# Linear attention and two mixture layers on one core: attention loads as four tiles four groups ahead, banks apart, weight splits in pieces

## Chip, cores and metric

One core of one Trainium2 chip. The metric is device microseconds of one execution. Five engines work from queues of their own: TensorE (PE; its weight loads are PEld), VectorE (DVE), ScalarE (ACT), GpSimd (POOL) and SyncE (SP), which here only issues transfers.

## The reference, cut to what matters

```python
for t in range(S):                                   # B, H, S, D = 4, 8, 768, 48
    cur = einsum('bhd,bhe->bhde', u * k[t], v[t])
    y[t] = einsum('bhd,bhde->bhe', r[t], state + cur)
    state = w[:, :, None] * state + einsum('bhd,bhe->bhde', k[t], v[t])
x = y.transpose(0, 2, 1, 3).reshape(3072, 384)
idx = argmax(normed(x) @ normed(expert_emb).T / tau)  # top-1 of 8 experts
out[idx == e] = gate * (relu(x[idx == e] @ w1[e]) @ w2[e])   # 384 -> 1024 -> 384
h = out @ w_in                                        # 384 -> 2048
y = (h * clip(h + 3, 0, 6) / 6) @ w_out               # 2048 -> 384
```

## The kernel before, in words

The sequence is cut into 6 chunks of 128 tokens (NCH), the 8 heads into 4 pairs (HP). A *group* is one pair of heads of one chunk for all 4 batches; there are 24, in the order of the loop at L709. Behind them come the experts, one after the other (`expert`, L473), and the last layer (L1091 on). The experts' weights are float32 and are split into a high and a low part (`prep_w`, L179: a CAST on ScalarE at L187, a subtraction at L190), so that each product is three matmuls (`mm3`, L388).

What one group i does, by helper:

- `load` (L519): two transfers by SyncE. `dt_t` (112 x 1536 floats: r, k and v with the head's dimension on the partitions) and `tk` (128 x 832: k and v with the token on the partitions). Both have three buffers.
- `scaled` (L609): `k_s` and `r_s` on VectorE, `rk_p` on GpSimd, `kk` on VectorE (not in the last chunk).
- `scores` (L622): 8 matmuls into two banks `a_ps`, copies by ScalarE (L632), a causal mask by GpSimd (L633) into `a_m`.
- `current` (L638): the matmul `m_ps` (L641), and `mv = m_ps * v` on VectorE (L643), which is the last reader of `dt_t`.
- `outputs` (L646): `y_ps` from the state (L652, not in the first chunk) and from `a_m` (L656), `u_ps` (L663), then `y_sb` (L665) and the new state (L670) on VectorE.
- `by_token` (L673): four transposes of `y_sb` into `x_ps` (L677), copied by ScalarE (L678).

In iteration i the loop issues the loads of group i+2, the scores and `m_ps` of i+1, the transposes of i-1, `scaled` of i+2 and the outputs of i. TensorE's instructions keep the order in which the program writes them (`pin`), and the others are placed by a scheduler when the program is built. Each engine works strictly in its order.

Every fourth group the routing of the chunk before is taken one step further (`route`, L203): `lt_ps` (L211), `l_ps` (L220) and a chain of small operations on VectorE that ends in `ohot` and `aft`, then ranks `r_ps` (L243 to L247) and counts `c_ps` (L251), and four scatters of rows by GpSimd (L266). At group 15 the biggest expert so far is chosen (`leader`, L317); SyncE reads its number (`lead_i`, L134) before it can ask for its weights (L173).

PSUM has 8 banks. During the attention `psM` has two, in turn for `m_ps`, `lt_ps`, `l_ps`, `r_ps`, `c_ps` and the transposes of `x_cols`; `a_ps` has two, `y_ps` two, `u_ps` and `x_ps` one each. The weights' transfers go through a staging pool of two buffers (`wst`); the first three are split at group 20 (L738).

Of the kernel before, what the change touches and what calls it, by code (L numbers as in the profile page):

```python
# [44 lines left out]
def rwkv_moe_kernel(ctx, tc, dT, tokA, wuT, uw, emb, tau, w1, w2, win, wout, out):  # L45
# [133 lines left out]
    def prep_w(j, lo_eng, after=None, st=None):  # L179
        if st is None:  # L180
            st = load_w(j)
        wp = wpools[(j // 4) % 2]
        hi = wp.tile([128, WCH], F32R, name="whi", tag="whi")
        lo = wp.tile([128, WCH], F32R, name="wlo", tag="wlo")
        for c0 in range(0, WCH, WCH // 3):
            sl = slice(c0, c0 + WCH // 3)
            cp = nc.scalar.copy(out=hi[:, sl], in_=st[:, sl])  # L187
            if after:
                behind(cp, after)
            sub = lo_eng.tensor_tensor(out=lo[:, sl], in0=st[:, sl], in1=hi[:, sl].bitcast(F32), op=ALU.subtract)  # L190
# [12 lines left out]
    def route(c, x_t, sm, xT, st_p, group="rows", pin=lambda i: i):  # L203
# [38 lines left out]
        r_ps = psM.tile([128, B, E], F32, name="r_ps", tag="m")  # L242
# [5 lines left out]
        c_ps = psM.tile([128, 2, E], F32, name="c_ps", tag="m")  # L248
# [257 lines left out]
    with actx:  # L506
        ld = actx.enter_context(tc.tile_pool(name="ld", bufs=3))
# [4 lines left out]
        yp = actx.enter_context(tc.tile_pool(name="yp", bufs=HP + 2))  # L512
# [6 lines left out]
        def load(c, hp):  # L519
            dt_t = ld.tile([112, 3, B, C], F32, name="dt_t", tag="dt")  # L520
            loads[c * HP + hp] = nc.sync.dma_start(out=dt_t, in_=dT[c, hp].rearrange("p (x b t) -> p x b t", x=3, b=B)).ins
            tk = ld.tile([128, B * 96 + B * 112], F32, name="tk", tag="tk", bufs=3)
            nc.sync.dma_start(out=tk, in_=tokA[c, hp][:, 2 * B * 96:])
            return dt_t, (tk[:, 0:B * 96].rearrange("p (b d) -> p b d", b=B), tk[:, B * 96:].rearrange("p (b d) -> p b d", b=B))
# [10 lines left out]
        for i in range(1, 2):  # L535
            data[i] = load(*groups[i])
# [72 lines left out]
        def scaled(c, hp, dt_t, tk):  # L609
            r_s = rk.tile([112, B, C], F32, name="r_s", tag="r", bufs=3)  # L610
            k_s = rk.tile([112, B, C], F32, name="k_s", tag="k")
            loads["k_s"] = nc.vector.tensor_tensor(out=k_s, in0=dt_t[:, 1], in1=itab[:, hp:hp + 1, :].to_broadcast([112, B, C]), op=ALU.mult).ins
            nc.vector.tensor_tensor(out=r_s, in0=dt_t[:, 0], in1=ptab[:, hp:hp + 1, 0:C].to_broadcast([112, B, C]), op=ALU.mult)
            rk_p = rk.tile([112, B, C], F32, name="rk_p", tag="ku")
            nc.gpsimd.tensor_tensor(out=rk_p, in0=dt_t[:, 0], in1=dt_t[:, 1], op=ALU.mult)
            kk = None
            if c < NCH - 1:
                kk = rk.tile([128, B, 96], F32, name="kk", tag="kk", bufs=3)
                nc.vector.tensor_tensor(out=kk, in0=tk[0], in1=ktab[:, hp:hp + 1, :].to_broadcast([128, B, 96]), op=ALU.mult)
            return r_s, k_s, rk_p, kk  # L620
# [17 lines left out]
        def current(c, hp, dt_t, rk_p):  # L638
# [7 lines left out]
        def outputs(c, hp, tk, r_s, a_sb, kk, mv):  # L646
            s_n, s_o = (state[hp][(c - i) % 2] for i in range(2))
            y_ps = psY.tile([112, B, C], F32, name="y_ps", tag="y")
            if c > 0:
                for b in range(B):  # L650
                    for p0, n in halves:
                        pin(nc.tensor.matmul(y_ps[p0:p0 + n, b, :], lhsT=s_o[p0:p0 + 48, b, 0:n], rhs=r_s[p0:p0 + 48, b, :],  # L652
                                             start=(b == 0), stop=False, skip_group_check=True))
            for b in range(B):
                for h2, (p0, n) in enumerate(halves):
                    pin(nc.tensor.matmul(y_ps[p0:p0 + n, b, :], lhsT=tk[1][:, b, p0:p0 + n], rhs=a_sb[h2][:, b, :],  # L656
                                         start=(c == 0), stop=True, skip_group_check=True))
# [24 lines left out]
        AHEAD = 2
# [26 lines left out]
        for i, (c, hp) in enumerate(groups):  # L709
# [12 lines left out]
            ys[i] = outputs(c, hp, data[i][1], r_s, a_sbs.pop(i), kk, mvs.pop(i))  # L722
# [6 lines left out]
            if c == KC and hp == 3:  # L729
# [468 lines left out]
```

## Time and profile before

| | |
|---|---|
| median of 3 runs | 863.66 us (862.76 to 864.56) |
| the profiled execution | 861.97 us, span 860.3 us |
| mean granted clock of TensorE | 0.962 |
| busy share of the span | PE 92%, PEld 82%, DVE 58%, ACT 39%, POOL 26% |
| first matmul of the first expert (L390) | 201.78 us |

The span begins with the first instruction. A busy share is a mean over stages with different limits, so each stage is read by itself: up to 201.78 us is the attention, behind it the experts. The clock is a share of TensorE's full speed.

### The profile page before, as it was taken

Reading aid. Unit: us, or ns where it says so; the run is one execution under the profiler, and the core shown is the slowest. Engines: PE = TensorE matmul, PEld = TensorE weight load, DVE = VectorE, ACT = ScalarE, POOL = GpSimd, SP = SyncE. Lnnn points to the kernel's source line nnn. Section 1 sums busy time; section 2 is a strip of 40 time slices with the busy share of each in tenths; the row PEclk is TensorE's granted clock in tenths of the full one; section 3 lists DMA queues with packets and bytes.
Section 4 is the critical chain, followed back from the end, with each engine's and each line's share of the span. In section 5 each row is a group of like instructions: output and inputs, shape, how many; then the busy total and the mean of one; then the engine's idle time right before and its main releaser. Section 6 shows DMA issues by size and latency. Waiting matters only on the chain. (4 is left out here: it accounts for less than half of the span.)

```text
span 860.3 us, 13475 instructions
## 1 busy us (share of the span) xinstructions
PE 792.6 (92%) x5178; PEld 703.9 (82%) x5179; DVE 495.9 (58%) x1014; ACT 331.9 (39%) x644; POOL 225.3 (26%) x239
## 2 busy tenths in 40 slices
PE   7678678598999999999999999999999999999994
PEld 4456556477899999999888998798998999998994
DVE  7764556766376778785948878744334334333331
ACT  3333132443355545564444433443333334333331
POOL 6645535564333224322110111121002002001001
PEclk8979798799999999999999999999999999999998
DMA  7556557842466465745322221111000001000000
GB/s 199 149 154 171 165 156 220 224 131 90 146 195 201 160 202 187 224 151 175 109 80 75 70 60 55 38 38 37 1 1 37 1 1 37 1 1 37 1 1 37
DMA packets 24024, 86.42 MB, mean 100 GB/s; under 512 B 3852, under 2 KB 5953, under 8 KB 23952
## 3 DMA queue, kind: packets, MB, share of 16 engines
q1 hardware_dynamic: 18784, 70.81, 27.4%
q0 software_dynamic: 5168, 14.68, 4.8%
q8 instruction: 42, 0.69, 0.3%
q14 instruction: 30, 0.25, 0.1%
HBM read 72.84 MB, written 12.63 MB: 99 GB/s over the span
## 5 line engine op out<-in xcount | busy, mean ns | idle before, releaser
L391 PE MATMUL l<-xl,whi 128*128 128x512 f32 (+8 forms) x504 | 186.8, 371 | 0.0
L390 PE MATMUL l<-xh,whi 128*128 128x512 f32 (+8 forms) x504 | 184.5, 371 | 2.0 <-DVEq L1057 1.7
L392 PE MATMUL l<-xh,wlo 128*128 128x512 f32 (+8 forms) x504 | 186.0, 370 | 0.0
L426 DVE SCALAR_TENSOR_TENSOR rg<-rg,l 128x512 f32<-128x512 f32 x96 | 65.8, 687 | 132.1 <-ACT rg L425 131.9
L425 ACT ACTIVATE rg<-l,nums 128x512 f32<-128x512 f32 x96 | 65.7, 688 | 170.8 <-PE l L392 160.2
L441 PE MATMUL o<-wlo,hh 128*128 128x384 f32 x384 | 128.7, 335 | 0.4 <-POOL wlo L1085 0.4
L440 PE MATMUL o<-whi,hh 128*128 128x384 f32 x384 | 128.1, 336 | 0.5 <-ACT hh L427 0.5
L442 PE MATMUL o<-whi,hl 128*128 128x384 f32 x384 | 123.9, 335 | 0.0
L390 PEld LDWEIGHTS l<-xh,whi 128*128 128x128 f32 x504 | 95.0, 190 | 13.4 <-issue 2.9
L392 PEld LDWEIGHTS l<-xh,wlo 128*128 128x128 f32 x504 | 95.4, 189 | 12.9
L391 PEld LDWEIGHTS l<-xl,whi 128*128 128x128 f32 x504 | 95.3, 189 | 10.1
L428 DVE TENSOR_TENSOR hl<-rg,hh 128x512 fp32r<-128x512 f32 x96 | 66.7, 696 | 43.7 <-ACT hh L427 43.1
L1115 POOL DMA_INDIRECT out_dram<-o_t,ctok x20 | 20.6, 1032 | 254.4 <-ACT o_t L1113 250.8
L427 ACT CAST hh<-rg 128x512 fp32r<-128x512 f32 x96 | 59.4, 621 | 67.4 <-DVE rg L426 52.5
L440 PEld LDWEIGHTS o<-whi,hh 128*128 128x128 f32 x384 | 72.0, 188 | 5.2 <-ACT hh L427 0.8
L441 PEld LDWEIGHTS o<-wlo,hh 128*128 128x128 f32 x384 | 72.1, 188 | 4.1 <-POOL wlo L1085 0.7
L391 PE MATMUL acc<-hl,whi 128*128 128x256 f32 (+7 forms) x216 | 71.8, 334 | 0.2 <-DVE hl L487 0.2
L392 PE MATMUL acc<-hh,wlo 128*128 128x256 f32 (+7 forms) x216 | 72.0, 335 | 0.0
L442 PEld LDWEIGHTS o<-whi,hl 128*128 128x128 f32 x384 | 71.7, 188 | 0.3
L487 DVE SCALAR_TENSOR_TENSOR hl<-l,hh 128x256 fp32r<-128x256 f32 (+7 forms) x72 | 38.1, 542 | 54.5 <-ACT hh L486 54.4
L486 ACT ACTIVATE hh<-l 128x256 fp32r<-128x256 f32 (+7 forms) x72 | 33.5, 480 | 92.5 <-PE l L392 89.7
L390 PE MATMUL acc<-hh,whi 128*128 128x256 f32 (+7 forms) x216 | 65.2, 335 | 0.7 <-DVE x L903 0.7
(215 smaller groups left out, 1191.5 us busy)
## 6 DMA issues: line engine op xcount, KB each, us to landing
wst<-in_w_dram SPq DMA_DIRECT2D x32, 768.0 KB, 4.3
dt_t<-in_dT_dram SPq DMA_DIRECT2D x24, 672.0 KB, 5.2
tk<-in_tok_dram SPq DMA_DIRECT2D x24, 416.0 KB, 5.5
q<-in_win_dram SPq DMA_DIRECT2D x16, 384.0 KB, 3.4
q<-in_wout_dram SPq DMA_DIRECT2D x16, 384.0 KB, 3.2
wf_d<-t SPq DMA_DIRECT2D x16, 192.0 KB, 4.1
wst<-wf_d SPq DMA_DIRECT2D x4, 768.0 KB, 4.6
rows<-xs_d,prod POOLq DMA_INDIRECT x27, 4.7
```

The source lines that it names most:

```text
L390: pin(nc.tensor.matmul(ps, lhsT=w[0], rhs=x[0], start=first, stop=False))
L391: pin(nc.tensor.matmul(ps, lhsT=w[0], rhs=x[1], start=False, stop=False))
L392: pin(nc.tensor.matmul(ps, lhsT=w[1], rhs=x[0], start=False, stop=last))
L425: nc.scalar.activation(out=r6, in_=ps, func=AF.Relu, bias=three)
L426: nc.vector.scalar_tensor_tensor(out=gf, in0=r6, scalar=6.0, in1=ps, op0=ALU.min, op1=ALU.mult)
L427: nc.scalar.copy(out=gh, in_=gf)
L428: nc.vector.tensor_tensor(out=gl, in0=gf, in1=gh.bitcast(F32), op=ALU.subtract)
L440: pin(nc.tensor.matmul(acc[t], lhsT=gh[:, sl], rhs=wh[:, f % 4, :], start=(f == span[0]), stop=False))
L441: pin(nc.tensor.matmul(acc[t], lhsT=gh[:, sl], rhs=wl[:, f % 4, :], start=False, stop=False))
L442: pin(nc.tensor.matmul(acc[t], lhsT=gl[:, sl], rhs=wh[:, f % 4, :], start=False, stop=(f == span[1] - 1)))
L486: last["a"] = nc.scalar.activation(out=hh[:, 0:n], in_=ps[:, 0:n], func=AF.Relu).ins
L487: last["v"] = nc.vector.scalar_tensor_tensor(out=hl[:, 0:n], in0=ps[:, 0:n], scalar=0.0, in1=hh[:, 0:n].bitcast(F32), op0=ALU.max, op1=ALU ...
```

## The change

- `load` issues four transfers a group in place of two: `rk_t` (r and k, 3 buffers), `tk` (k by token, 3), `vd` (v by dimension, 5) and `vt` (v by token, 5), with the same bytes in all. They are requested four groups ahead in place of two, the first four groups before the loop.
- `m_ps` gets a pool `psW` of one bank; `y_ps` has one bank in place of two.
- `c_ps` becomes a part of the bank of `r_ps`.
- The first four weight transfers stand behind the loads of groups 20 to 23 (before: 12 to 15). The splits of the first three chunks are nine pieces, two each at groups 18, 19, 20 and 22 and one at 23, ordered behind `x_t` on ScalarE and behind `y_sb` on VectorE.
- `yp` has one buffer fewer.

```diff
-        behind(dma, 12 + j if j < 4 else HP * NCH - 1)
+        behind(dma, (20, 21, 22, 23)[j] if j < 4 else HP * NCH - 1)
...
-        for c0 in range(0, WCH, WCH // 3):
+
+        def piece(c0):
             sl = slice(c0, c0 + WCH // 3)
             cp = nc.scalar.copy(out=hi[:, sl], in_=st[:, sl])
             if after:
...
+            if after == "x_t":
+                behind(sub, "y_s")
+        for c0 in range(0, WCH, WCH // 3):
+            if later is None:
+                piece(c0)
+            else:
+                later.append(lambda c0=c0: piece(c0))
...
-        r_ps = psM.tile([128, B, E], F32, name="r_ps", tag="m")
+        rc_ps = psM.tile([128, B + 2, E], F32, name="r_ps", tag="m")
+        r_ps, c_ps = rc_ps[:, 0:B], rc_ps[:, B:]
...
-        c_ps = psM.tile([128, 2, E], F32, name="c_ps", tag="m")
...
-        psY = pa.enter_context(tc.tile_pool(name="psY", bufs=2, space=PSUM))
+        psY = pa.enter_context(tc.tile_pool(name="psY", bufs=1, space=PSUM))
+        psW = pa.enter_context(tc.tile_pool(name="psW", bufs=1, space=PSUM))
...
-            dt_t = ld.tile([112, 3, B, C], F32, name="dt_t", tag="dt")
-            loads[c * HP + hp] = nc.sync.dma_start(out=dt_t, in_=dT[c, hp].rearrange("p (x b t) -> p x b t", x=3, b=B)).ins
-            tk = ld.tile([128, B * 96 + B * 112], F32, name="tk", tag="tk", bufs=3)
-            nc.sync.dma_start(out=tk, in_=tokA[c, hp][:, 2 * B * 96:])
...
+            rk_t = ld.tile([112, 2, B, C], F32, name="rk_t", tag="rk", bufs=3)
+            loads[c * HP + hp] = nc.sync.dma_start(out=rk_t, in_=dT[c, hp][:, 0:2 * B * C].rearrange("p (x b t) -> p x b t", x=2, b=B)).ins
+            tk = ld.tile([128, B, 96], F32, name="tk", tag="tk", bufs=3)
+            nc.sync.dma_start(out=tk, in_=tokA[c, hp][:, 2 * B * 96:3 * B * 96].rearrange("p (b d) -> p b d", b=B))
+            vd = ld.tile([112, B, C], F32, name="vd", tag="vd", bufs=5)
+            nc.sync.dma_start(out=vd, in_=dT[c, hp][:, 2 * B * C:].rearrange("p (b t) -> p b t", b=B))
+            vt = ld.tile([128, B, 112], F32, name="vt", tag="vt", bufs=5)
+            nc.sync.dma_start(out=vt, in_=tokA[c, hp][:, 3 * B * 96:].rearrange("p (b d) -> p b d", b=B))
...
-        for i in range(1, 2):
+        for i in range(1, 4):
             data[i] = load(*groups[i])
...
-            m_ps = psM.tile([112, B, C], F32, name="m_ps", tag="m")
+            m_ps = psW.tile([112, B, C], F32, name="m_ps", tag="w")
...
-            nc.vector.tensor_tensor(out=mv, in0=m_ps, in1=dt_t[:, 2], op=ALU.mult)
+            nc.vector.tensor_tensor(out=mv, in0=m_ps, in1=vd, op=ALU.mult)
...
-        AHEAD = 2
+        AHEAD = 4
...
+            if i in (16, 17, 20):
+                j = (16, 17, 20).index(i)
+                chunks[j] = prep_w(j, nc.vector, "x_t", load_w(j), pieces)
+            for _ in range((0, 0, 2, 2, 2, 0, 2, 1)[i - 16] if i >= 16 else 0):
+                pieces.pop(0)()
             if i == 20:
                 x0 = x_cols(rows0, NE, e0p, NE)
-                for j in range(3):
-                    chunks[j] = prep_w(j, nc.vector)
+            if i == 21:
                 st3 = load_w(3)
```

In the built programs the instructions move as follows (the changed kernel's line numbers are 8 to 13 higher for the same operation).

SyncE's queue, requests for loads in the middle of the attention; the number behind a tile's name tells its buffers apart. Before:

```order
L521 DMA dt_t_1176<-in_dT_dram 112x1536
L523 DMA tk_1076<-in_tok_dram 128x832
L521 DMA dt_t_1249<-in_dT_dram 112x1536
L523 DMA tk_1178<-in_tok_dram 128x832
L521 DMA dt_t_1333<-in_dT_dram 112x1536
```

With the change, at the place where the leader's number is read (`vd`, `rk_t`, `vt`, `tk` are the four parts of a group's load; `vt` is of the group before the others):

```order
L534 DMA vd_1718<-in_dT_dram 112x512
L530 DMA rk_t_1714<-in_dT_dram 112x1024
L536 DMA vt_1615<-in_tok_dram 128x448
L532 DMA tk_1716<-in_tok_dram 128x384
L134 TENSOR_LOAD lead_i_136
L134 ISA x2
L173 ISA
L173 DMA wst_1802<-in_w1_dram 128x1536
L534 DMA vd_1820<-in_dT_dram 112x512
L532 DMA tk_1818<-in_tok_dram 128x384
L530 DMA rk_t_1816<-in_dT_dram 112x1024
```

Four requests stand where two stood, the weights' first request has moved behind the loads of more groups, and the read of `lead_i` stands ahead of the parts of group 20.

VectorE, one group without routing, before:

```order
L612 TENSOR_TENSOR k_s<-dt_t,itab 112x512
L619 TENSOR_TENSOR kk<-tk,ktab 128x384
L643 TENSOR_TENSOR mv<-m_ps,dt_t 112x512
L613 TENSOR_TENSOR r_s<-dt_t,ptab 112x512
L665 TENSOR_TENSOR y_sb<-y_ps,mv 112x512
L670 SCALAR_TENSOR_TENSOR state_1_232<-state_0_231,ptab,u_ps 112x4x48
```

With the change:

```order
L632 TENSOR_TENSOR kk<-tk,ktab 128x384
L625 TENSOR_TENSOR k_s<-rk_t,itab 112x512
L656 TENSOR_TENSOR mv<-m_ps,vd 112x512
L626 TENSOR_TENSOR r_s<-rk_t,ptab 112x512
L678 TENSOR_TENSOR y_sb<-y_ps,mv 112x512
L683 SCALAR_TENSOR_TENSOR state_1_259<-state_0_258,ptab,u_ps 112x4x48
```

`kk` has moved from behind `k_s` to ahead of it, so that `mv` stands right behind `k_s`; the other four keep their places.

ScalarE, the splits of the first two weight chunks, before:

```order
L632 COPY a_m<-a_ps 128x512 x2
L678 COPY x_t<-x_ps 128x4x96
L187 CAST whi<-wst 128x512 x3
L632 COPY a_m<-a_ps 128x512 x2
L187 CAST whi<-wst 128x512 x3
L678 COPY x_t<-x_ps 128x4x96
```

With the change:

```order
L645 COPY a_m<-a_ps 128x512 x2
L691 COPY x_t<-x_ps 128x4x96
L188 CAST whi<-wst 128x512 x2
L645 COPY a_m<-a_ps 128x512 x2
L691 COPY x_t<-x_ps 128x4x96
L188 CAST whi<-wst 128x512 x2
L645 COPY a_m<-a_ps 128x512 x2
L691 COPY x_t<-x_ps 128x4x96
```

Three and three casts stood together around a group's copies of `a_ps`; now two stand behind each group's `x_t`.

## Rows read from the trace of the kernel before

**Rows 1.** Stages: window, length, busy us (instructions) of PE, PEld, DVE, ACT, POOL, clock, DMA, GB/s.

```profile
30.94:68.47 37.53, 25.56 (x295) 19.33 (x293) 23.05 (x50) 9.91 (x24) 21.37 (x18) 0.82 0.51 147
...
102.68:136.62 33.94, 24.86 (x310) 19.07 (x308) 20.46 (x56) 9.17 (x22) 17.40 (x18) 0.85 0.54 156
136.62:172.73 36.11, 26.69 (x311) 20.47 (x309) 25.37 (x61) 14.73 (x33) 19.48 (x19) 0.83 0.86 239
172.73:201.78 29.05, 26.35 (x315) 19.13 (x315) 14.88 (x38) 11.61 (x28) 16.60 (x19) 0.98 0.38 120
201.78:240.00 38.22, 35.28 (x288) 34.04 (x285) 19.73 (x75) 16.81 (x45) 12.52 (x15) 0.96 0.39 127
240.00:400.00 160.00, 160.00 (x884) 154.04 (x883) 121.13 (x231) 81.01 (x163) 50.58 (x41) 1.00 0.59 191
```

**Rows 2.** TensorE's timeline, one chunk of four groups: start, us, engine, line, operation, idle before.

```profile
102.68 1.16 PE L629 MATMUL a_ps<-r_s,k_s 48*128 48x128 f32 x16
...
105.20 1.08 PE L652 MATMUL y_ps<-r_s,state 48*64 48x128 f32 x16
...
107.68 1.16 PE L629 MATMUL a_ps<-r_s,k_s 48*128 48x128 f32 x16
...
113.68 1.16 PE L629 MATMUL a_ps<-r_s,k_s 48*128 48x128 f32 x16
116.30 1.11 PE L641 MATMUL m_ps<-rk_p,ub 112*112 112x512 f32 x2 [1.46 <-DVE mv L643]
...
118.01 0.60 PE L220 MATMUL l_ps<-ident,lt 128*128 128x128 f32 x4
...
121.03 1.16 PE L629 MATMUL a_ps<-r_s,k_s 48*128 48x128 f32 x16
123.88 1.11 PE L641 MATMUL m_ps<-rk_p,ub 112*112 112x512 f32 x2 [1.69 <-DVE mv L643]
126.35 0.98 PE L677 MATMUL x_ps<-ident,y_sb 112*128 112x112 f32 x4 [1.35 <-DVE ohot L234]
...
131.90 0.25 PE L251 MATMUL c_ps<-ohot,ones 128*128 128x8 bf16 x4 [4.38 <-DVE mv L643]
...
132.19 1.97 PE L652 MATMUL y_ps<-r_s,state 48*64 48x128 f32 x16
...
136.62 1.16 PE L629 MATMUL a_ps<-r_s,k_s 48*128 48x128 f32 x16
```

**Rows 3.** Timeline of SyncE's queue: one request for loads in that chunk.

```profile
116.31 0.31 SPq L521 DMA_DIRECT2D dt_t<-in_dT_dram  x1
```

**Rows 4.** VectorE's timeline behind that request.

```profile
121.00 0.69 DVE L612 TENSOR_TENSOR k_s<-dt_t,itab 112x512 f32<-112x512 f32 x1 [2.93 <-DMA dt_t<-in_dT_dram]
121.83 1.40 DVE L619 TENSOR_TENSOR kk<-tk,ktab 128x384 f32<-128x384 f32 x1
123.15 0.68 DVE L643 TENSOR_TENSOR mv<-m_ps,dt_t 112x512 f32<-112x512 f32 x1
```

**Rows 5.** What SyncE's queue waited for, 0 to 240 us: us in total, times, longest.

```profile
SPq L521 <- DVE mv L643: 119.1, 21, 12.3
```

**Rows 6.** Groups by line, 0 to 200 us: busy us, mean ns of one, idle before.

```profile
L615 POOL TENSOR_TENSOR rk_p<-dt_t 112x512 f32<-112x512 f32 x24 | 41.9, 1744 | 49.8 <-DMA dt_t<-in_dT_dram 40.0 <-PE u_ps L663 3.5 <-PE y_ps L656 3.3
L633 POOL TENSOR_SCALAR_AFFINE_SELECT a_m<-a_m 128x512 f32<-128x512 f32 x48 | 38.3, 806 | 22.6 <-ACT a_m L632 22.4
...
L613 DVE TENSOR_TENSOR r_s<-dt_t,ptab 112x512 f32<-112x512 f32 x24 | 23.1, 963 | 10.6 <-DMA dt_t<-in_dT_dram 6.2 <-PE y_ps L652 4.4
L266 POOL DMA_INDIRECT xs_d<-x_t,dsti x20 | 21.3, 1067 | 9.5 <-issue 4.6 <-DVE wrk L279 1.1 <-DVE wrk L280 1.1
```

**Rows 7.** DMA queues of the whole span: packets, MB, share of 16 engines.

```profile
q1 hardware_dynamic: 18784, 70.81, 27.4%
q0 software_dynamic: 5168, 14.68, 4.8%
```

**Rows 8.** DMA issues, 0 to 240 us: KB each, median us to landing.

```profile
wut<-in_wuT_dram SPq DMA_DIRECT2D x1, 5.2 KB, 1.6
```

More of the change, by code (lines that the diff above doesn't have):

```diff
@@ L177, in load_w, with prep_w @@
         return st
-    def prep_w(j, lo_eng, after=None, st=None):
+    def prep_w(j, lo_eng, after=None, st=None, later=None):
         if st is None:
@@ L607, in rwkv_moe_kernel, with scaled @@
         halves = ((0, 64), (64, 48))
-        def scaled(c, hp, dt_t, tk):
+        def scaled(c, hp, rk_t, tk, vd, vt):
             r_s = rk.tile([112, B, C], F32, name="r_s", tag="r", bufs=3)
             k_s = rk.tile([112, B, C], F32, name="k_s", tag="k")
-            loads["k_s"] = nc.vector.tensor_tensor(out=k_s, in0=dt_t[:, 1], in1=itab[:, hp:hp + 1, :].to_broadcast([112, B, C]), op=ALU.mult).ins
-            nc.vector.tensor_tensor(out=r_s, in0=dt_t[:, 0], in1=ptab[:, hp:hp + 1, 0:C].to_broadcast([112, B, C]), op=ALU.mult)
+            loads["k_s"] = nc.vector.tensor_tensor(out=k_s, in0=rk_t[:, 1], in1=itab[:, hp:hp + 1, :].to_broadcast([112, B, C]), op=ALU.mult).ins
+            nc.vector.tensor_tensor(out=r_s, in0=rk_t[:, 0], in1=ptab[:, hp:hp + 1, 0:C].to_broadcast([112, B, C]), op=ALU.mult)
             rk_p = rk.tile([112, B, C], F32, name="rk_p", tag="ku")
-            nc.gpsimd.tensor_tensor(out=rk_p, in0=dt_t[:, 0], in1=dt_t[:, 1], op=ALU.mult)
+            nc.gpsimd.tensor_tensor(out=rk_p, in0=rk_t[:, 0], in1=rk_t[:, 1], op=ALU.mult)
             kk = None
@@ L618, in scaled @@
                 kk = rk.tile([128, B, 96], F32, name="kk", tag="kk", bufs=3)
-                nc.vector.tensor_tensor(out=kk, in0=tk[0], in1=ktab[:, hp:hp + 1, :].to_broadcast([128, B, 96]), op=ALU.mult)
+                nc.vector.tensor_tensor(out=kk, in0=tk, in1=ktab[:, hp:hp + 1, :].to_broadcast([128, B, 96]), op=ALU.mult)
             return r_s, k_s, rk_p, kk
@@ L636, in scores, with current, outputs @@
             return a_sb
-        def current(c, hp, dt_t, rk_p):
-            m_ps = psM.tile([112, B, C], F32, name="m_ps", tag="m")
+        def current(c, hp, vd, rk_p):
+            m_ps = psW.tile([112, B, C], F32, name="m_ps", tag="w")
             pin(nc.tensor.matmul(m_ps, lhsT=ub[:, hp, :], rhs=rk_p, start=True, stop=True))
             mv = rk.tile([112, B, C], F32, name="mv", tag="mv")
-            nc.vector.tensor_tensor(out=mv, in0=m_ps, in1=dt_t[:, 2], op=ALU.mult)
+            nc.vector.tensor_tensor(out=mv, in0=m_ps, in1=vd, op=ALU.mult)
             return mv
-        def outputs(c, hp, tk, r_s, a_sb, kk, mv):
+        def outputs(c, hp, vt, r_s, a_sb, kk, mv):
             s_n, s_o = (state[hp][(c - i) % 2] for i in range(2))
@@ L655, in outputs @@
                 for h2, (p0, n) in enumerate(halves):
-                    pin(nc.tensor.matmul(y_ps[p0:p0 + n, b, :], lhsT=tk[1][:, b, p0:p0 + n], rhs=a_sb[h2][:, b, :],
+                    pin(nc.tensor.matmul(y_ps[p0:p0 + n, b, :], lhsT=vt[:, b, p0:p0 + n], rhs=a_sb[h2][:, b, :],
                                          start=(c == 0), stop=True, skip_group_check=True))
@@ L662, in outputs @@
                         d0 = 48 if p0 else 0
-                        pin(nc.tensor.matmul(u_ps[p0:p0 + n, b, :], lhsT=kk[:, b, d0:d0 + n], rhs=tk[1][:, b, p0:p0 + 48], start=True, stop=True))
+                        pin(nc.tensor.matmul(u_ps[p0:p0 + n, b, :], lhsT=kk[:, b, d0:d0 + n], rhs=vt[:, b, p0:p0 + 48], start=True, stop=True))
             y_s = yp.tile([112, B, C], F32, name="y_sb", tag="y")
-            nc.vector.tensor_tensor(out=y_s, in0=y_ps, in1=mv, op=ALU.add)
+            loads["y_s"] = nc.vector.tensor_tensor(out=y_s, in0=y_ps, in1=mv, op=ALU.add).ins
             if c < NCH - 1:
@@ L677, in by_token @@
                 pin(nc.tensor.transpose(x_ps[:, b, 0:112], y_s[:, b, :], ident[0:112, 0:112]))
-            nc.scalar.copy(out=x_t[:, :, hp * 96:hp * 96 + 96].rearrange("p b (h d) -> p b h d", d=D),
-                           in_=x_ps.rearrange("p b (h d) -> p b h d", d=64)[:, :, :, 0:48])
-        pend, rest = None, []
-        AHEAD = 2
+            loads["x_t"] = nc.scalar.copy(out=x_t[:, :, hp * 96:hp * 96 + 96].rearrange("p b (h d) -> p b h d", d=D),
+                           in_=x_ps.rearrange("p b (h d) -> p b h d", d=64)[:, :, :, 0:48]).ins
+        pend, rest, pieces = None, [], []
+        AHEAD = 4
         def prepare(i):
@@ L693, in begin @@
                 a_sbs[i] = scores(r_s, k_s)
-                mvs[i] = current(*groups[i], data[i][0], rk_p)
+                mvs[i] = current(*groups[i], data[i][2], rk_p)
         def moved(i):
@@ L721, in rwkv_moe_kernel @@
             r_s, _, _, kk = pre.pop(i)
-            ys[i] = outputs(c, hp, data[i][1], r_s, a_sbs.pop(i), kk, mvs.pop(i))
+            ys[i] = outputs(c, hp, data[i][3], r_s, a_sbs.pop(i), kk, mvs.pop(i))
             for _ in range(min(2, len(rest))):
```

6 lines of the change are left out of this document (3 added, 3 removed).

## The prediction

> **What bounds the kernel now.** I read the stages first, then TensorE's timeline of one chunk, then what stands behind its waits. Behind the attention TensorE is full: 160.00 of 160.00 us busy from 240 to 400 us, and 35.28 of 38.22 us in the stage before that [rows 1]. The change touches nothing there, so what the attention saves reaches the end nearly whole. In the attention it is otherwise: 24.86 of 33.94 us, at a granted clock of 0.85 [rows 1].
>
> The timeline shows why. From one group's scores to the next TensorE takes 5.00 us (102.68 to 107.68) when nothing is late, and 6.00 us with `lt_ps` (107.68 to 113.68) [rows 2]. Then come waits: 1.46 and 1.69 us of `m_ps` for `mv`, 1.35 us for `ohot`, 4.38 us of `c_ps` for `mv`, 8.88 us in all [rows 2]. After the last one the clock has fallen: from the state product at 132.19 to the next scores takes 4.43 us, where the same stretch took 2.48 us from 105.20 to 107.68 [rows 2].
>
> All these waits hang on one loop. `dt_t` is only free when `mv` has read it, so SyncE's queue waits for `mv` 21 times, 119.1 us in all [rows 5]. A request at 116.31 [rows 3] is followed by a `k_s` that waited for its load until 121.00; `kk` and `mv` stand behind it on VectorE, and `mv` ends at 123.83 [rows 4], when the next request can go: 7.5 us a turn, 4.7 of them the transfer. `c_ps` and `m_ps` share two banks, so TensorE waits for the same late `mv`.
>
> **The change, part by part.**
>
> *Loads as four tiles, four groups ahead.* `mv` now frees only `vd`, which has five buffers; `rk_t` is free after `scaled`, which runs two groups before its scores. A request then stands about two group times ahead of its use, over 10 us, against 4.7 us for a transfer. The loop is gone, and with it 1.46 + 1.69 us of a chunk and the late `ohot` (1.35 us). The price: two more issues a group on SyncE at 0.31 us each [rows 3], on an engine that does nothing else; and 480 rows in place of 240 for the same 1.114 MB (112 x 1536 and 128 x 832 floats). By bytes a group needs 4.0 us of DMA: 239 GB/s at a share of 0.86 [rows 1] is 278 GB/s at full share. With the scatters (0.2 MB a group) it is 4.7 us, below what TensorE needs.
>
> *Banks.* `c_ps` no longer waits for a bank of `m_ps`: 4.38 us, and with the wait the low clock behind it, 1.95 us a chunk (4.43 less 2.48) [rows 2]. The one bank of `m_ps` makes it wait for the `mv` of the group before. In the new order `mv` stands before `y_sb`, with the outputs and the next scores on TensorE in between, so it costs nothing while VectorE is less than some 3 us late. The one bank of `y_ps` costs nothing: the transposes ahead of it on TensorE already wait for the `y_sb` that frees it.
>
> *What is late next.* TensorE itself. The floor of a chunk is 5.0 + 6.0 + 5.6 (with `l_ps`, 0.60) + 5.6 us (eight `c_ps` matmuls took 0.29 us from 131.90 to 132.19, and `r_ps` has as many), 22.2 us [rows 2]. The other way round, 33.94 less 8.88 and 1.95 is 23.1 us. I take 22.5. Two things are added. GpSimd has four scatters in a row between the two masks of a group; at 1.07 us [rows 6] and some gap that is 4.3 to 5.5 us by which the second mask is late, while some 4 us of other work lie before its reader. I take 2 us a chunk, between 0 and 5.5. And VectorE and GpSimd disturb each other: `kk` takes 1.40 us [rows 4] beside `rk_p`, though it is smaller than `k_s` with 0.69. Their busy times, 20.46 and 17.40 us a chunk [rows 1], stay below 22.5, so this shows only where the two meet at a bad moment: 1 us, between 0 and 4. A chunk then takes **25.5 us**.
>
> The Trainium skill (SBUF — State Buffer, "SBUF: two separate sides") says that VectorE operations with two SBUF inputs and GpSimd's hold an exclusive lock on one pair of ports, and that the loser fully blocks. The stretched `kk` agrees; by that rule met at every group the sum would be that of the port rival below.
>
> *The weights.* Their splits no longer stand in threes around the copies of `a_ps`. That the stage from 136.62 took 36.11 us and not 34 [rows 1] is theirs, and I count it as gone. SyncE now waits for `lead_i` ahead of group 20's loads; these have two group times to spare. The fourth chunk has some 1.6 MB of weights more to load, 5.7 us of DMA at 278 GB/s, beside 18.8 us for its own: 24.5, just under its 25.5.
>
> *Start and tail.* The first four groups end at 30.94 us; their first loads are asked for in the same order, so I give them 30 (27 to 33). The last 29.05 us run at a clock of 0.98 already [rows 1]; five split pieces come in, the last two behind `y_sb` on VectorE: 30 (27 to 33).
>
> **Sum.** 30 + 4 x 25.5 + 30 = 162 us for the attention, against 201.78 [rows 1]: 39.8 us less. The profiled execution took 861.97 us (span 860.3), so it would take 822.2. It lies 1.7 us below the median of the runs, 863.66, and the forecast for the median is **824 us**. With both ends at every place the attention takes between 27 + 90 + 27 = 144 us and 33 + 4 x 32 + 33 = 194; the waits excluded above are not likely to come all at once, and a chunk of 24 to 28 us gives 818 to 834.
>
> **The rivals.**
>
> - *TensorE's floor.* Nothing is added to 22.2 us a chunk: 30 + 88.8 + 28 = 146.8, a gain of 55, 809 us. For it: TensorE ran two groups without any wait [rows 2]. Against it: these followed a stall in which the others got ahead.
> - *DMA by rows.* If a row costs as much as now whatever its length, the loads' 201 ns (27.4% of 16 x 860.3 us over 18784 packets) make 6.0 us of a group's 480 rows, and the scatters' 128 ns (4.8% over 5168) 1.0 us for 128 rows [rows 7]: 7.0 a group, 28.2 a chunk, 173 in all, 835 us. Against it: the scatters' packets are smaller and cost less, so the price goes by bytes.
> - *The port.* Every group VectorE waits out one `rk_p` and one mask, 1.74 + 0.81 us [rows 6], on top of 20.46 / 4 = 5.1: 7.7 a group, 30.6 a chunk, 182 in all, 844 us. `r_s` with a mean of 0.96 [rows 6] against 0.69 for `k_s` [rows 4] says that this is now met in part.
> - *The change does not do what it says.* SyncE's queue is one line; a request that waits for `kk` or `u_ps` holds back those behind it. If loads come no earlier than now, the loop of 7.5 us stays and only the bank's wait goes: 30 a chunk, 180 in all, 842 us. The new order of the requests speaks against it.
> - *Slower: a fixed price per transfer.* The smallest transfer, 5.2 KB, landed after 1.6 us [rows 8]. If that part of each transfer of the one queue stood by itself, a group would need 4 x 1.6 + 4.0 = 10.4 us, 24 groups 250 us, and with 14 us for the last groups' work the attention would take 264: 62 us more, 926 us. It decides from 1.1 us on, (8.5 - 4.0) / 4. Against it: the stage from 136.62 moved 8.6 MB (239 GB/s) [rows 1] in some 12 requests in 36.11 us; at 1.6 us each it would have taken 50. The Trainium skill (SBUF — State Buffer, "The DMA setup-cost knee") has a fixed cost of about 2 us per transfer and asks to coalesce, which speaks against four tiles; the trace shows that price only where a transfer is waited for.
>
> **How the numbers follow.** Forecast 0.70 (818 to 834), floor 0.08, DMA by rows 0.08, port 0.07, not earlier 0.04, slower 0.03. The range takes in the forecast, the floor's edge and the row rival: 809 to 838. Some 0.2% is what a measurement of this kernel tells from no change. All cases but the last lie more than 1% below: faster 0.96, same 0.01, slower 0.03.
>
> **What would show it.** Right: the first `l` of L390's operation near 162 us; chunks of some 25 us; `k_s` and `rk_p` no longer waiting for DMA; `c_ps` without a wait; a granted clock of 0.95 or more in the attention; the stages behind it as long as now. Wrong: SyncE's queue still waiting for the last readers while `k_s` waits for loads; a DMA share near 1 in every chunk; `y_ps` or `m_ps` waiting for masks or `mv` at every group; or, behind the attention, TensorE waiting for weights.

## The result and the profile after

The changed kernel takes **823.86 us** (median of 4 runs, 820.93 to 824.43) where the kernel before takes 863.77 beside it: a ratio of 0.9532, 95% interval 0.9507 to 0.9557. The profiled execution took 824.2 us (span 822.4); TensorE's mean granted clock is 0.981. The first matmul of the first expert stands at 162.14 us, where it stood at 201.78.

The stages of the changed kernel, columns as in [rows 1]; a chunk is counted from its first scores to those of the next, the last two rows lie behind the attention:

```profile
9.17:32.73 23.56, 19.16 (x185) 14.51 (x184) 21.95 (x30) 7.30 (x19) 15.65 (x14) 0.86 1.04 293
32.73:53.64 20.91, 20.91 (x295) 16.20 (x294) 16.05 (x45) 9.94 (x24) 11.77 (x14) 1.00 0.78 223
53.64:75.46 21.82, 21.82 (x311) 16.95 (x309) 19.48 (x43) 9.29 (x22) 17.87 (x18) 1.00 0.77 233
75.46:98.47 23.01, 22.01 (x310) 16.87 (x309) 19.61 (x40) 9.18 (x22) 17.11 (x18) 1.00 0.76 231
98.47:131.08 32.61, 27.26 (x310) 20.66 (x309) 21.97 (x72) 11.24 (x26) 20.83 (x23) 0.85 0.77 234
131.08:162.14 31.06, 27.52 (x316) 19.62 (x315) 18.84 (x47) 14.94 (x35) 17.13 (x18) 0.94 0.28 93
162.14:200.36 38.22, 33.15 (x272) 31.86 (x269) 19.35 (x74) 14.96 (x41) 12.79 (x14) 0.96 0.37 119
200.36:360.36 160.00, 160.00 (x890) 154.00 (x889) 120.97 (x232) 82.92 (x167) 50.94 (x41) 1.00 0.59 191
```

The first two chunks are TensorE alone: busy 20.91 of 20.91 and 21.82 of 21.82 us. Then the gain stops: the fourth chunk takes 32.61 us, at a clock of 0.85. From the attention's end to the end of the span it is 660.3 us (822.4 less 162.14), before 658.5 (860.3 less 201.78).

TensorE's timeline of the third chunk, which answers to [rows 2]:

```profile
75.46 1.16 PE L642 MATMUL a_ps<-r_s,k_s 48*128 48x128 f32 x16
80.46 1.16 PE L642 MATMUL a_ps<-r_s,k_s 48*128 48x128 f32 x16
86.45 1.16 PE L642 MATMUL a_ps<-r_s,k_s 48*128 48x128 f32 x16
91.89 1.16 PE L642 MATMUL a_ps<-r_s,k_s 48*128 48x128 f32 x16
...
95.10 0.57 PE L690 MATMUL x_ps<-ident,y_sb 112*128 112x112 f32 x4 [1.00 <-DVE ohot L242]
```

Groups take 5.00, 5.99 and 5.44 us; of the four waits of [rows 2] the one for `ohot` is left, and `c_ps` has none. The waits of SyncE's queue for its loads, 0 to 200 us (us in total, times, longest), answer to [rows 5]:

```profile
...
SPq L530 <- POOL rk_p L628: 15.9, 6, 3.5
SPq L530 <- DVE r_s L626: 15.7, 12, 2.1
...
SPq L534 <- DVE mv L656: 10.4, 8, 2.6
```

In place of 119.1 us for `mv` there are short waits for several readers. The groups by line, 0 to 160 us, columns as in [rows 6], and the loads' queue, as in [rows 7]:

```profile
L628 POOL TENSOR_TENSOR rk_p<-rk_t 112x512 f32<-112x512 f32 x24 | 32.3, 1347 | 6.1 <-DMA rk_t<-in_dT_dram 3.1 <-PE m_ps L654 1.9 <-POOL a_m L646 0.9
L625 DVE TENSOR_TENSOR k_s<-rk_t,itab 112x512 f32<-112x512 f32 x24 | 23.1, 963 | 1.5 <-PE a_ps L642 1.4
L626 DVE TENSOR_TENSOR r_s<-rk_t,ptab 112x512 f32<-112x512 f32 x24 | 21.4, 891 | 7.8 <-PE y_ps L665 7.7
L656 DVE TENSOR_TENSOR mv<-m_ps,vd 112x512 f32<-112x512 f32 x24 | 16.3, 681 | 6.6 <-PE m_ps L654 6.6
L632 DVE TENSOR_TENSOR kk<-tk,ktab 128x384 f32<-128x384 f32 x20 | 13.7, 688 | 0.1
L268 DVE TENSOR_SCALAR gate<-gate 128x4 f32<-128x4 f32 x5 | 2.7, 548 | 0.0
```

```profile
q1 hardware_dynamic: 25312, 70.81, 28.2%
```

`rk_p` waited 40.0 us for loads, now 3.1; `k_s` no longer waits for them, where in the kernel before (VectorE's waits, 30 to 202 us) it did ten times:

```profile
DVE k_s L612 <- DMA dt_t<-in_dT_dram: 22.2, 10, 4.1
```

A packet of q1 takes 147 ns (28.2% of 16 x 822.4 us over 25312), before 201.

In the fourth chunk, by the timelines of GpSimd, ScalarE, VectorE and TensorE:

```profile
111.05 1.10 POOL L373 DMA_INDIRECT rows<-xs_d,ix  x1 [3.15 <-DMA xs_d<-x_t,dsti]
...
115.94 1.05 POOL L206 TENSOR_TENSOR ny<-ss,nums 128x4 f32<-128x4 f32 x1
...
117.02 0.17 DVE L207 TENSOR_SCALAR ny<-ny 128x4 f32<-128x4 f32 x1 [5.09 <-POOL ny L206]
...
118.15 0.61 ACT L384 ACTIVATE rows<-rows 128x384 f32<-128x384 f32 x1 [7.33 <-DMA rows<-xs_d,ix]
...
120.23 1.05 ACT L645 COPY a_m<-a_ps 128x512 f32<-128x512 f32 x2
...
120.84 2.56 PE L642 MATMUL a_ps<-r_s,k_s 48*128 48x128 f32 x16 [3.40 <-ACT a_m L645]
```

The first expert's rows are gathered here and in no other chunk (L373, two transfers). GpSimd waits 3.15 us for the scatters before it can ask for them; the masks and `ny` stand behind that, and VectorE stands 5.09 us for `ny`. ScalarE's scaling of the rows (L384) waits 7.33 us, and a group's copies of `a_ps` stand behind it. After TensorE's wait of 3.40 us the scores take 2.56 us in place of 1.16: the granted clock is 0.60 over them, and 0.50 from 123.40 us to the end of the chunk.

### The profile page after: what moved, and what is told of

Same layout as the page of the kernel before. It is cut to its first block, busy times and chain, and to the rows that moved or that the text cites. A ratio compares the mean times of both kernels' runs of the same rounds, so it can differ in the third digit from the quotient of the medians.

```text
span 822.4 us, 13576 instructions
## 1 busy us (share of the span) xinstructions
PE 784.0 (95%) x5178; PEld 698.3 (85%) x5179; DVE 494.7 (60%) x1014; ACT 331.7 (40%) x644; POOL 218.9 (27%) x239
## 3 DMA queue, kind: packets, MB, share of 16 engines
q1 hardware_dynamic: 25312, 70.81, 28.2%
## 5 line engine op out<-in xcount | busy, mean ns | idle before, releaser
L398 PEld LDWEIGHTS l<-xh,whi 128*128 128x128 f32 x504 | 94.9, 189 | 13.4 <-issue 2.8
```

The source lines that it names most:

```text
L398: pin(nc.tensor.matmul(ps, lhsT=w[0], rhs=x[0], start=first, stop=False))
```

## The experiments

The kernel before measured 863.77, 867.55, 866.59, 869.12 and 870.10 us on the chips used, so kernels of different chips are compared by their ratio to it. This table is worked out from the timelines: the start of the scores of group 4, the four chunks and the tail between the scores of groups 4, 8, 12, 16, 20 and the first expert's matmul, and the ratio with its interval. Starts, chunks and tails are those of one execution each, the ratios those of medians.

```
                  start  1st    2nd    3rd    4th    tail   end     ratio
before            30.94  37.53  34.21  33.94  36.11  29.05  201.78
changed           32.73  20.91  21.82  23.01  32.61  31.06  162.14  0.9532 0.9507-0.9557
changed again     29.56  21.30  22.54  26.68  30.32  31.84  162.24  0.9532 0.9496-0.9569
loads alone       30.64  21.42  22.44  28.08  33.10  28.51  164.19  0.9515 0.9471-0.9560
banks alone       34.12  29.88  33.07  34.53  34.70  33.32  199.62  0.9930 0.9896-0.9965
old splits        31.24  20.92  21.81  23.07  33.63  30.70  161.37  0.9491 0.9447-0.9534
two ahead         31.52  20.92  21.81  24.97  32.12  31.58  162.92  0.9512 0.9465-0.9559
halves            27.88  23.15  27.64  22.74  33.33  33.23  167.97  0.9526 0.9485-0.9566
rows late         29.86  21.47  21.82  23.20  30.14  29.21  155.70  0.9493 0.9449-0.9536
gather late       30.85  20.92  22.65  25.37  27.82  33.19  160.80  0.9465 0.9427-0.9504
route late        30.84  21.17  25.01  25.75  27.56  34.69  165.02  0.9486 0.9452-0.9520
third bank        31.90  21.17  26.66  25.36  25.22  32.47  162.78  0.9487 0.9451-0.9522
rk_p on VectorE   32.77  20.97  22.02  22.88  35.17  31.59  165.40  0.9549 0.9503-0.9595
both              33.53  20.92  22.44  26.26  26.57  29.21  158.93  0.9485 0.9445-0.9525
```

### Which part carries the gain

**Loads alone**: the banks, weight requests and splits of the kernel before, the loads of the changed one.

```diff
-        m_ps = psW.tile(..., tag="w")
+        m_ps = psM.tile(..., tag="m")
...
+        c_ps = psM.tile([128, 2, E], F32, name="c_ps", tag="m")
...
-        behind(dma, (20, 21, 22, 23)[j] ...)
+        behind(dma, 12 + j ...)
```

> The loads alone: four tiles, four groups ahead, with the banks and the weights' requests and splits of the kernel before. Theory A (the late mv was the root of all the waits): once mv is early, c_ps finds its bank free, and most of the gain stays: 824 to 834. Theory B (the banks carry their own part): c_ps still waits 4.38 us a chunk and the clock falls behind it, four times 6.3 us stay: 846 to 852.

827.29 us; the whole gain within the interval. Theory A held. TensorE's waits in its attention (us in total, times, longest):

```profile
PE c_ps L259 <- DVE mv L655: 4.5, 5, 3.1
```

4.5 us in all, where the kernel before has 4.38 in one chunk [rows 2]: the bank was late because `mv` was late.

**Banks alone**: the same lines the other way round, in the kernel before.

> The banks alone: m_ps and y_ps with one bank each, c_ps in the bank of r_ps, with the loads (two tiles, two groups ahead) and weights of the kernel before. Theory A (the loads' loop of 7.5 us a group is the root): without the wait of c_ps TensorE waits for the next k_s instead, a chunk goes from 34 to between 30 and 33 us: 845 to 862. Theory B (the banks carry their own part): c_ps' 4.38 us and the low clock behind it go, 6.3 us a chunk: 836 to 842.

860.8 us, 6.75 below the kernel before on the same chip. Theory A's time held, at the small end, though two chunks (34.53 and 34.70 us) lie above the 30 to 33 that it gave: SyncE waits as before [rows 5], and VectorE for the loads:

```profile
SPq L522 <- DVE mv L644: 126.2, 21, 12.8
```

```profile
DVE k_s L613 <- DMA dt_t<-in_dT_dram: 33.6, 16, 3.8
```

**Old splits**: the changed kernel with the weights' requests behind groups 12 to 15 and three splits together at group 20.

> The changed kernel, with the weights' requests and splits as before: requests behind the loads of groups 12 to 15, three splits together at group 20. Theory: what the pieces brought is about what the prediction counted, 2.1 us (36.11 less 34): 825 to 829. Rival: the fourth chunk of the changed kernel is long because of the pieces and of the weights' requests, so with the old ones it falls to some 25 us: 815 to 819. Second rival: the early requests stand in SyncE's queue ahead of the loads and wait there for the leader's number, so that loads come late: 830 to 840.

824.77 us, ratio 0.9491: not slower than the changed kernel at all, and its fourth chunk is as long (33.63 us). Neither the theory's 2.1 us nor a rival shows: the order of the weights decides nothing that these runs can tell. Beside "loads alone", which differs from it by the banks only, it is 2.5 us faster on the same chip. That is the most likely worth of the banks once the loads are early, but the runs overlap (822.76 to 825.55 and 824.20 to 829.07), so it is not clear of noise.

**Two ahead**: `AHEAD = 2`, four tiles and all buffers kept, the weights' first two requests behind groups 18 and 19.

> The changed kernel with the loads asked for two groups ahead in place of four (two groups before the loop in place of four), four tiles and all buffers kept; the weights' first two requests then stand behind the loads of groups 18 and 19. Theory A (what matters is that a tile is free earlier, since rk_t is read two groups before mv): a request still goes out a group before its use, 4.7 us of transfer hide in 5.4 us of a group, and the time is within 4 us of the changed kernel. Theory B (the distance of four groups matters): k_s waits for its load at each group again, some 2 us a group, 20 groups: 850 to 870.

825.04 us beside 826.69 for the changed kernel, so theory A's time held. But the edit did not shorten the distance. By the timelines of SyncE and VectorE a request of `rk_t` stands 13.28 us ahead of the `k_s` that reads it (median of groups 8 to 23), in the changed kernel 13.38; in the kernel before it is 5.55 us for `dt_t`, in "loads alone" 14.27. One group's request and its `k_s`, in the changed kernel and here:

```profile
83.37 0.33 SPq L530 DMA_DIRECT2D rk_t<-in_dT_dram  x1
...
97.36 0.97 DVE L625 TENSOR_TENSOR k_s<-rk_t,itab 112x512 f32<-112x512 f32 x1
```

```profile
82.17 0.33 SPq L530 DMA_DIRECT2D rk_t<-in_dT_dram  x1
...
96.49 0.98 DVE L625 TENSOR_TENSOR k_s<-rk_t,itab 112x512 f32<-112x512 f32 x1
```

A request goes out when a buffer is free, whichever of the two numbers the program has. `rk_t` has three buffers, as `dt_t` had; it now waits for `rk_p` and `r_s` and not for `mv`. So the separate release is what put these requests further ahead, and this run can't weigh a distance of two groups against four. Whether more buffers for the undivided `dt_t` would do the same, or `vd` and `vt` need their five, was not tried.

**Halves**: eight transfers a group, rows of half the length.

```diff
-            vd: one dma_start of [112, B, C]
+            vd: two dma_starts of [112, B/2, C]; rk_t, tk, vt alike
```

> The changed kernel with each of the four transfers of a group cut into two, each with rows of half the length: eight transfers a group and twice the rows for the same bytes. Theory (transfers overlap and the price goes by bytes): within 2 us of the changed kernel, save up to 4 us in the start, which is bound by DMA. Rival 1 (a fixed price per transfer in one line, 1.6 us): 8 x 1.6 + 4.0 = 16.8 us a group, over 1000 us. Rival 2 (a price per row of 153 ns whatever its length): 960 rows a group make 9.2 us of 16 engines, 24 groups 220 us: 885 to 905.

826.47 us beside 826.69 (the table's trace is of its slowest execution, 829.57). Both rivals fall. Its queue:

```profile
q1 hardware_dynamic: 38368, 70.81, 29.2%
```

A packet now takes 101 ns (29.2% of 16 x 827.8 us over 38368) after 147 (the expectation said 153): the price goes by bytes, and transfers of one queue overlap. The Trainium skill (SBUF — State Buffer, "The DMA setup-cost knee") gives each transfer about 2 us of its own; no such price shows here, where nothing waits for the single transfer.

### What holds the fourth chunk

**Changed again**: the changed kernel with no edit, the measure for the next kernels.

> The changed kernel once more, unchanged, as the measure for the other kernels beside it. Expected: 822 to 828, first expert's matmul at 160 to 164 us of the span, and the fourth chunk again longer than the third by some 9 us.

826.69 us. The fourth chunk (30.32 us) is 3.6 us longer than the third, not some 9: the third came out at 26.68 us where the first trace has 23.01, from the same program. The stages of that chunk show where (columns as in [rows 1]), and the timeline the wait ahead of it:

```profile
73.40:91.00 17.60, 17.45 (x238) 13.23 (x238) 12.15 (x27) 7.50 (x18) 13.98 (x15) 1.00 0.80 229
91.00:94.10 3.10, 1.45 (x8) 0.41 (x6) 3.00 (x13) 0.79 (x3) 0.53 (x2) 0.99 0.43 124
94.10:100.08 5.98, 5.94 (x69) 5.50 (x69) 5.95 (x27) 0.88 (x2) 3.80 (x4) 0.50 0.65 186
```

```profile
94.14 0.98 PE L690 MATMUL x_ps<-ident,y_sb 112*128 112x112 f32 x4 [1.35 <-DVE ohot L242]
```

TensorE waited 1.35 us for `ohot` where the first trace has 1.00, and after it the granted clock is 0.50 up to the next chunk; in the first trace it stayed at 1.00. So a single chunk can differ by 3.7 us from one execution to the next, and the medians decide.

**Rows late**: the scalings of the gathered rows behind group 19's `x_t` on ScalarE.

```diff
-                x0 = x_cols(rows0, NE, e0p, NE)
+                x0 = x_cols(rows0, NE, e0p, NE, after="x_t")
```

> The changed kernel, with the two scalings of the gathered rows (rows, L384) put behind group 19's copy of x_t on ScalarE instead of behind the routing's squares four groups earlier. Nothing else moves on TensorE, GpSimd or SyncE. Theory: the fourth chunk (98.47 to 131.08 us, 32.61 us) is long because ScalarE's queue stands 7.33 us behind the gather, ahead of a group's copies of a_ps, and because TensorE's clock falls behind that wait; then the fourth chunk comes to 24 to 26 us and the time to 815 to 819. Rival: it is long for the routing's scatters, masks and weights' transfers, which stay: the fourth chunk stays at 31 to 33 us and the time at 822 to 826.

823.43 us, ratio 0.9493; the fourth chunk takes 30.14 us. ScalarE's wait is gone, but the time lies in the rival's range and is not told apart from the changed kernel's, and the chunk lies between the two forecasts. GpSimd's and VectorE's part is still there, as the timelines show:

```profile
108.90 1.10 POOL L373 DMA_INDIRECT rows<-xs_d,ix  x1 [3.13 <-DMA xs_d<-x_t,dsti]
...
114.87 1.84 DVE L207 TENSOR_SCALAR ny<-ny 128x4 f32<-128x4 f32 x1 [5.07 <-POOL ny L206]
...
118.47 1.42 PE L654 MATMUL m_ps<-rk_p,ub 112*112 112x512 f32 x2 [2.08 <-DVE mv L656]
```

**Gather late**: beside that, the gather behind `ny` on GpSimd.

```diff
-                rows0 = x_rows(NE, e0p, ix0, KC * B * C)
...
+            if i == 17:
+                rows0 = x_rows(NE, e0p, ix0, KC * B * C, "ny")
```

> Of the earlier kernel with only the scalings of the rows moved, the fourth chunk still took 30.14 us: there GpSimd's gather of the rows stood ahead of the routing's ny (L206) and of two masks, and waited 3.13 us for the scatters; VectorE stood 5.07 us behind ny, and mv, y_sb and ohot behind that. Here the gather stands behind ny too, and the scalings behind group 19's copy of x_t. Theory (two queues, ScalarE's and GpSimd's, stood behind the one gather): the fourth chunk falls to 22 to 25 us, the attention ends at 147 to 152 us of the span, and the time is 9 to 14 us below the changed kernel beside it. Rival (the weights' transfers and the read of the leader's number by SyncE, which stay): the chunk stays at 29 us or more, and the time is at most 4 us below.

820.45 us, 6.2 below the changed kernel beside it (826.69), ratio 0.9465 against 0.9532: the fastest kernel of this study, though the two intervals touch. The fourth chunk falls to 27.82 us: under the rival's 29, but not to the theory's 25. The theory had the right queue but not all of it. The tail is longer (33.19 us), so in this trace the attention ends only 1.4 us before that of "changed again" (160.80 and 162.24). The timelines of GpSimd, VectorE and TensorE show what is left:

```profile
117.66 0.64 POOL L649 TENSOR_SCALAR_AFFINE_SELECT a_m<-a_m 128x512 f32<-128x512 f32 x1
117.69 1.88 DVE L236 TENSOR_SCALAR sel<-lg 128x32 f32<-128x32 f32 x1
118.28 1.25 POOL L631 TENSOR_TENSOR rk_p<-rk_t 112x512 f32<-112x512 f32 x1
...
121.67 0.98 PE L693 MATMUL x_ps<-ident,y_sb 112*128 112x112 f32 x4 [2.93 <-DVE ohot L242]
```

`sel` takes 0.18 us where GpSimd is idle; here it starts beside a mask and ends with the `rk_p` behind it. TensorE then waits 2.93 us for `ohot`, and its granted clock is 0.50 from there to the end of the chunk.

The kernels below that keep the gather late say the same: in the four traces with it the fourth chunk takes 25.22 to 27.82 us, in the eight of the changed kernel and its variants without it 30.14 to 35.17, and the four ratios (0.9465 to 0.9487) lie below the eight others (0.9491 to 0.9549), though each interval alone is wider than that gap.

**rk_p on VectorE**: the changed kernel with `rk_p` there.

```diff
-            nc.gpsimd.tensor_tensor(out=rk_p, ...)
+            nc.vector.tensor_tensor(out=rk_p, ...)
```

> The changed kernel with the product rk_p (L628) on VectorE in place of GpSimd, to measure what VectorE loses beside GpSimd. Theory (operations of VectorE that read SBUF alone stand still while GpSimd works, those that read PSUM don't): k_s falls from a mean of 0.96 to under 0.80 us, kk from 0.69 to under 0.60, and the routing's small operations of 1.2 to 1.9 us are gone or halved; VectorE gains 0.6 us a group by that and pays 0.69 us for each rk_p, so the time is within 4 us of the changed kernel, ratio 0.949 to 0.958. Rival (the stretch has another cause, such as its own queue): k_s and kk stay as long, VectorE has 22.3 us of work in a chunk of 21.8 and becomes the bound: ratio above 0.960.

829.57 us, ratio 0.9549: inside the theory's range. VectorE's groups, 0 to 160 us:

```profile
L628 DVE TENSOR_TENSOR rk_p<-rk_t 112x512 f32<-112x512 f32 x24 | 18.5, 771 | 0.4 <-DMA rk_t<-in_dT_dram 0.4
L625 DVE TENSOR_TENSOR k_s<-rk_t,itab 112x512 f32<-112x512 f32 x24 | 17.9, 744 | 4.1 <-PE a_ps L642 2.1 <-PE x_ps L690 2.0
L626 DVE TENSOR_TENSOR r_s<-rk_t,ptab 112x512 f32<-112x512 f32 x24 | 17.3, 721 | 6.6 <-PE y_ps L665 5.0 <-DMA rk_t<-in_dT_dram 1.3 <-PE y_ps L669 0.3
L656 DVE TENSOR_TENSOR mv<-m_ps,vd 112x512 f32<-112x512 f32 x24 | 16.4, 685 | 5.9 <-PE m_ps L654 3.6 <-DMA wst<-in_w_dram 2.2
L632 DVE TENSOR_TENSOR kk<-tk,ktab 128x384 f32<-128x384 f32 x20 | 11.1, 556 | 2.3 <-DMA tk<-in_tok_dram 2.2
L268 DVE TENSOR_SCALAR gate<-gate 128x4 f32<-128x4 f32 x5 | 0.8, 163 | 0.0
```

`k_s` falls from 963 to 744 ns, `r_s` from 891 to 721, `kk` from 688 to 556, `gate` from 548 to 163; `mv`, which reads PSUM, stays (681 and 685). So `rk_p` on GpSimd had stretched these and not `mv`. For `k_s`, `r_s` and `kk` that is 0.52 us a group (0.22, 0.17 and 0.13), and `rk_p` itself costs VectorE 0.77: no gain in the time. The masks stay on GpSimd, so what they stretch is not in the 0.52.

**Both**: gather late, and `rk_p` on VectorE.

> The kernel with gather and scalings moved, and rk_p on VectorE. There VectorE lost 1.7 us at one small operation of the fourth chunk (sel, L236, 1.88 us beside a mask and rk_p) and 1 us at k_s, and ohot came 2.93 us late. Theory (what is left of the fourth chunk's loss is GpSimd's queue and its hold on VectorE): with rk_p gone from GpSimd the fourth chunk falls to 22 to 25 us, the attention ends at 147 to 155 us, ratio to the kernel before 0.935 to 0.944. Rival (VectorE's own work is the bound there: some 23 us with the leader's operations, and rk_p adds what the hold gives back): the fourth chunk stays at 26 us or more, ratio 0.945 to 0.955.

824.85 us, ratio 0.9485, the fourth chunk 26.57 us: the rival held. That VectorE's own work is what stands in the way then is the rival's reading; the numbers agree with it but do not show it. The third chunk is as long (26.26).

**Route late**: gather late, and the routing's second and third step behind a group's outputs.

```diff
-            if pend:
+            if pend and hp == 0:
                 step(pend, 1)
             ys[i] = outputs(...)
+            if pend and hp:
+                got = step(pend, 1)
```

> The kernel with gather and scalings moved, and beside that the routing's second and third step (l_ps, and r_ps with c_ps) behind a group's outputs on TensorE in place of ahead of them; on VectorE y_sb, the state and kk then stand ahead of the routing's small operations. Theory: TensorE waits 1.0 to 2.9 us for ohot in every chunk, because y_sb stands behind those small operations and r_ps right behind y_sb's transposes, and its clock falls at some of these waits, in one execution and not in another; with the new order the wait is gone, the third chunk takes 21.8 to 22.5 us, the fourth 22 to 25, the attention ends at 145 to 152 us, and the ratio to the kernel before falls to 0.933 to 0.942. Rival (VectorE as a whole is the bound in the fourth chunk, through GpSimd's hold on it): the fourth chunk stays at 27 us or more and the ratio at 0.945 to 0.949, that of the kernel with only the gather and the scalings moved.

826.07 us, ratio 0.9486. The fourth chunk stays at 27.56 us, as the rival said, and the theory falls: the clock is 1.00 in the second and third chunk, but they take 25.01 and 25.75 us. Other waits took the place of the one for `ohot` (TensorE, 30 to 166 us):

```profile
PE y_ps L672 <- POOL a_m L649: 2.3, 2, 1.2
PE y_ps L672 <- POOL x_t L718: 2.3, 2, 1.8
...
PE r_ps L252 <- DVE ohot L242: 2.1, 2, 1.2
```

The scatters now stand in GpSimd's queue ahead of other masks, and the outputs wait for these.

**Third bank**: beside that, the second transpose of the gathered rows in the bank of `m_ps`.

```diff
-            tp = psM.tile([128, NB], F32, name="tp", tag="m")
+            tp = (psW if k == 1 else psM).tile(...)
```

> As the kernel beside it with the routing's steps late, and the second of the three transposes of the first expert's rows (tp) in the bank of m_ps, so that the three have three banks. Theory: the third tp's wait for xl (1.33 to 2.05 us) goes, and with it the low clock that followed in some executions (3 us): 1.5 to 5 us below the kernel beside it. Rival (the wait goes over to the next m_ps, which has that bank): within 1 us of it.

825.1 us beside 826.07: within 1 us, as the rival said. `tp`'s wait for `xl`, 2.3 us in "route late", is gone from the trace, but the time did not follow: the fourth chunk and the tail are shorter by 2.3 and 2.2 us, the start and the second chunk longer by 1.1 and 1.7.

## Why the prediction was right, and where its steps were off

**The sum.** 162 us for the attention were forecast, and 162.14 and 162.24 measured. The stages behind it are as long as before: 38.22 us, and 160 of 160 us busy. The cause was right, but that the sum came out so close is luck. In the first trace three chunks lie 10.8 us under their forecast, the fourth 7.1 over it, and start and tail 3.8 over.

- *Loads.* Right, and nearly all of the gain: loads alone have a ratio of 0.9515. "Over 10 us" from request to use is what the trace shows, 13.38 us where it was 5.55, and `k_s` no longer waits for its load. It was not the four in the program that brought this: with two in its place the requests go out as early.
- *Banks.* The prediction gave 4.38 + 1.95 us of a chunk to the bank of `c_ps`. Loads alone and banks alone show that this wait was the late `mv` over again; the banks add perhaps 2.5 us in all. Since the sum took both away, nothing was counted twice. The 1.95 us of low clock were put behind the wrong wait: the clock had fallen before the 4.38 us began, at the 1.35 us for `ohot` (the kernel before, columns as in [rows 1]):

```profile
126.35:127.30 0.95, 0.95 (x10) 0.91 (x11) 0.78 (x5) 0.36 (x1) 0.57 (x1) 0.50 1.06 325
```

- *The chunk's floor and what is added.* The floor of 22.2 us held (21.82 in the second chunk). The 2 us for scatters ahead of masks and 1 us for the port didn't come in the first two chunks: VectorE has 19.48 us of work in 21.82, and I take it that the slack hides them. The third takes 23.01 us in one trace and 26.68 in the other. The first three chunks together took 65.74 us in place of 76.5.
- *The weights: the step that failed.* "That the stage from 136.62 took 36.11 us and not 34 is theirs, and I count it as gone." With the old splits the changed kernel isn't slower (0.9491). The extra stayed and grew, from 2.1 us to 7.1 over the forecast of 25.5. What stands there in its place is, in part, the gather of the first expert's rows and its queues: moving it took the chunk from 32.61 and 30.32 us to 27.82. The granted clock of 0.95 that the prediction named as a sign is met in the first three chunks (1.00) and not in the fourth and the tail (0.85, 0.94). The prediction named the leader's number, but not the gather on GpSimd nor the scalings on ScalarE.
- *Start and tail.* 32.73 and 31.06 us in place of 30 and 30, inside their ranges. The start runs at a DMA share of 1.04 (293 GB/s).
- *Transfers and rows.* Two more requests a group cost nothing, as said; 147 ns a packet in place of 201 settles the row rival, and the halves the price per transfer.

**The rivals.** TensorE's floor came true in the first two chunks. That the change does not do what it says falls with SyncE's waits. The port's price was too high: taking `rk_p` off GpSimd shortens VectorE's operations by 0.52 us a group, where the rival charged 1.74 for it and 2.55 with the mask, and the time does not show it.

**What stays open.** Of the fourth chunk's 8.5 to 10.8 us over the second (30.32 and 32.61 less 21.82), 2.5 to 4.8 go with the gather's place. The rest I could not settle: VectorE has more to do there (72 instructions in place of 43, the leader's among them), GpSimd's hold hits some of them, and TensorE's clock falls behind waits. The routing's steps, `rk_p` and a bank were moved, and other waits came. Leaving the leader's operations out was not tried.

## What to carry to other kernels

When one reader of a tile is late by its nature, give the parts of the tile buffers of their own: a load goes out when its buffer is free, and here that put it 13.4 us ahead of its use in place of 5.6, while the number of groups ahead that the program asks for changed nothing. Before you credit a distance, measure it from request to use. Where one stage of a repeating pattern is longer than the others, look for work that happens only there, on every in-order queue, before you name a cause. Where several engines have little slack, a wait that you take away can come back at another place, so count the slack of all engines in the stage, not the waits of one.

## What the runs showed of the hardware

- VectorE's operations with two SBUF inputs, and `sel` and `gate` with one, can stand still while GpSimd runs a mask or `rk_p`, even through two of these in a row: `sel`, 0.18 us, took 1.88 beside a mask and `rk_p`. `mv`, which reads PSUM, took 681 ns on average with `rk_p` on GpSimd and 685 without. Not everything that reads SBUF alone is held: in the changed kernel a `gate` took 1.23 us beside `rk_p` (at 96.01), the reciprocal behind it 0.18 beside a mask (97.27), and a `k_s` beside two scatters 0.69 (103.09). The Trainium skill (SBUF — State Buffer, "SBUF: two separate sides") has the pair of ports as an exclusive lock for the whole instruction, for operations in a two-port mode and, against a GpSimd operation that reads SBUF, for those with two SBUF inputs; the trace agrees for `k_s`, `r_s` and `kk`. Whether `gate` (548 ns on average, 163 without `rk_p` on GpSimd) and `sel` ran in a two-port mode no run here shows.
- The length of one wait doesn't tell whether TensorE's clock falls behind it. In the kernel before, waits of 1.46 and 1.69 us left the granted clock at 1.00, and the next, 1.35 us, brought it to 0.50, 1.2 GHz. In the changed kernel it stayed at 1.00 after 1.00 us for `ohot` in one trace, and after 1.35 us at the same place in the other it was 0.50 for the next 5.98 us.
- Cutting each transfer in two left 70.81 MB at 29.2% of the DMA engines' time in place of 28.2%.
